# x transposed through DRAM and VectorE, attention's transfers in one piece: one change to a fused layer kernel

## The chip, the cores and the metric

The kernel runs on one core of a Trainium2 chip. TensorE (PE) multiplies, VectorE (DVE) and ScalarE (ACT) work on tensors in SBUF and PSUM, GpSimd (POOL) on SBUF alone, and the DMA queues of SyncE (SP) and ScalarE move data between DRAM and SBUF over 16 DMA engines. The metric is the time of one execution on the device, in microseconds; lower is better.

## The reference

S = 2048 rows of D = 512 are normalized, go through a local attention with 32 heads of 16 (each row looks at itself and the rows 2, 4, ... 14 before it) and through a gated feed-forward part with F = 1792:

```python
def _A_ref(x, wqkv, wo):
    H = 32; Dh = D // H; W, dil = 8, 2
    q, k, v = (x @ wqkv) split into (3, H, Dh)
    idx = pos[:, None] - (jnp.arange(W) * dil)[None, :]
    logits = jnp.einsum("bhsd,bhswd->bhsw", q, k[idx]) * Dh ** -0.5
    logits = jnp.where(idx >= 0, logits, -1e9)
    o = jnp.einsum("bhsw,bhswd->bhsd", softmax(logits), v[idx])
    return o.reshape(B, S, D) @ wo

def _B_ref(x, w1, b1, w2, b2):
    r = relu(x @ w1 + b1)
    return (r * r) @ w2 + b2

xn = _layernorm(x)
out = x + _A_ref(xn, wqkv, wo) * silu(_B_ref(xn, w1, b1, w2, b2))
```

(The code is shortened: reshapes, transposes and the batch of 1 are left out.)

## The kernel before

**Precision.** Each float32 product is made of three products of float32r parts: `high` copies a value rounded to float32r on ScalarE, `low` subtracts it from the value on VectorE or Pool, `split` does both (L105 to L113). `PASSES` (L34) lists the pairs high by high, high by low, low by high.

**Tiles.** A tile t is 128 rows (16 tiles), a chunk c is 4 tiles (512 rows), an attention unit u is 2 tiles (256 rows, 8 units).

**Phase 1** (L435 to L541) goes over the tiles. `mean` and `spread` (L342, L347) get a tile's statistics by ScalarE passes whose full-size result goes to a `scratch` tile in SBUF; `norm(t)` (L354) writes the normalized `xn` and calls `load_x(t + 4)`. `trans(t)` (L373) transposes `xn` on TensorE, four 128x128 blocks into PSUM `pxT`, and ScalarE copies the high part to `xt`; `lowx(t)` (L381) subtracts the low part from PSUM on VectorE. `qkv` (L385) then does 12 products for each of q, k and v, copies the result to `stg` on ScalarE and stores it to DRAM (`sq`, `sk`, `sv`). For tiles 4 to 15 both parts of `xt` are spilled to DRAM `sx` (L538); chunk 0's stay in SBUF (`xT`). At step t of the loop (L507) the code calls `norm(t + 3)`, q's products, `trans(t + 2)`, `spread(t + 4)`, k's products, `mean(t + 5)`, `lowx(t + 2)`, v's products and the spill, in this order. The w1 and w2 blocks of the first six f are loaded and split on the way (`load_w`, `split_w`).

**Phase 2** (L544 to L700) goes over the chunks and, in each, over 14 blocks f of F. `up(c, f)` (L407) is 12 products, then ScalarE makes relu and two squares, and `lowh(f)` (L423) makes the low part on VectorE; `down` (L547) multiplies two f later into four accumulators `pb`. `load_xT` (L400) brings the next chunk's `xT` back from `sx` on ScalarE's DMA queue as soon as the last `up` of a chunk is issued; there is one buffer for it. Between the last `up` of a chunk and the first of the next, TensorE does `down` of f = 11 (12 products), two `out_product` (24), and `down` of f = 12. `gate` adds the bias and applies silu; `trans_o`, `out_product` and `finish` make the attention's output product, multiply and store.

**Attention** (L202 to L292) runs on VectorE beside all this. A unit's q, k and v come from DRAM by `load_u` (L191): the heads lie in 4 groups g, and group g has the partitions 32g to 32g + 31, so each transfer is made of four DMAs over 32 partitions; `store` (L255) writes the result to `so` the same way. Per unit there are 4 products with k (`qk`) and 4 with v (`av`), each a 2048-wide multiplication and reduction, and the softmax.

**What sets the order.** All instructions of the engines keep the order in which the code issues them (`Ordered`, L62); DMAs from SP are not bound to it and are placed by the framework's planner. The code keeps two clocks, one for TensorE and one for VectorE (L49), and adds a price for every instruction: 227 ns a product, 150 a transpose, VectorE's elements at 0.96 per ns and 170. `pump(margin)` (L297) issues the next pieces of attention while VectorE's clock is at most `margin` after TensorE's: LATE = 3000 ns in phase 1, ROOM = 1000 ahead of each `lowh`, -SLACK = -500 elsewhere. `not_before` moves VectorE's clock up to a time at which an operand can be there.

Of the kernel before, what the change touches and what calls it, by code (L numbers as in the profile page):

```python
# [44 lines left out]
def body(ctx: ExitStack, tc: tile.TileContext, x, wqkv, wo, w1, b1, w2, b2, out):  # L45
# [117 lines left out]
    zero = px.tile([HALO, 4, P], F32, name="zero")  # L163

    def constants():
        G.memset(zero, 0.0)
        for t in (sk, sv):
            dma(t[:, :HALO, :].rearrange("g h c -> h g c"), zero)
        G.memset(mask, 0.0)
        for g in range(4):  # L170
            for blk in (1, 0):
                for w in range(W):
                    n = max(0, min(BI, (W - 1 - w) * DIL - blk * BI))
                    if n:
                        G.memset(mask[32 * g:32 * g + blk + 1, :n, w], -1e9)
# [8 lines left out]
    sx = {c: dram.tile([P, TPC, 2, KT, P], F32, name=f"sx{c}") for c in range(1, NCH)}  # L184
# [6 lines left out]
    def load_u(what, u):  # L191
        n = BI if what == "q" else WIN
        src = dict(q=sq, k=sk, v=sv)[what]

        t = att.tile([P, n, P], F32, name=f"{what}{u}", tag="k" if (what, u) == ("v", NU - 1) else what)
        for g in range(4):
            row = src[g, u * UP:u * UP + 1, :]
            ap = bass.AP(tensor=row.tensor, offset=row.offset, ap=[[BI * P, NB], [1, n * P]])
            dma(t[32 * g:32 * g + 32].rearrange("p i c -> p (i c)"), ap)
        return t  # L200

    def attention():  # L202
# [52 lines left out]
        def store(u):  # L255
            v = tiles.pop(("v", u))
            for g in range(4):
                dst = so[g, u * UP:(u + 1) * UP, :].rearrange("(n i) c -> n i c", i=BI)
                dma(dst, v[32 * g:32 * g + 32, :BI, :])
            done_units[0] = u + 1  # L260
# [66 lines left out]
    mv, means, rs, shifts, xn, pTs, xt, xT, seen = {}, {}, {}, {}, {}, {}, {}, {}, {}  # L327
# [11 lines left out]
    def scratch(t):  # L339
        return px.tile([P, D], F32, name=f"scratch{t}", tag="scratch")  # L340
# [13 lines left out]
    def norm(t):  # L354
        xn[t] = px.tile([P, D], F32, name=f"xn{t}", tag="xn", bufs=2)
        if t < 2:
# [10 lines left out]
    def place(t):  # L367
        if t < TPC:
            xt[t] = xT[0][:, t]
        else:  # L370
            xt[t] = pxT.tile([P, 2, KT, P], FR, name=f"xt{t}", tag="xt", bufs=4)

    def trans(t):  # L373
        place(t)
# [63 lines left out]
    high(*wq_parts(0, 0))  # L438
    V.bn_stats(sts[1], xins[1])
    norm(0)  # L440
    moments(1, sts[1])
    low(*wq_parts(0, 0), V)
    high(*wq_parts(0, 1))
    low(*wq_parts(0, 1), G)
    xT[0] = xTa.tile([P, TPC, 2, KT, P], FR, name="xT0", tag="xT")
    place(0)
# [5 lines left out]
    for kt in (0, 2):  # L452
# [3 lines left out]
        V.tensor_sub(lo, src, hi.bitcast(F32))  # L456
    norm(1)
    for kt in (2, 3):
        split(*wq_parts(0, kt), V)
# [10 lines left out]
    def first():  # L470
        trans(1)
        highs(1, 0)

# [5 lines left out]
    mean(2)  # L479
# [27 lines left out]
    for t in range(2, NT):  # L507
# [14 lines left out]
        if t + 5 < NT:  # L522
            mean(t + 5)
# [6 lines left out]
        if t + 2 < NT:  # L530
            lowx(t + 2)
# [5 lines left out]
        if t >= TPC:  # L537
            dma(sx[t // TPC][:, t % TPC], xt.pop(t).bitcast(F32))  # L538
# [70 lines left out]
    for c in range(NCH):  # L609
# [3 lines left out]
        for f in range(2, NF):  # L613
# [51 lines left out]
            pump(ROOM)  # L665
# [4 lines left out]
        if not last:  # L670
            for i in range(2):
# [50 lines left out]
```

## Time and profile before

| | us |
|---|---|
| time, median of 3 runs | 509.35 |
| lowest and highest of them | 506.99, 510.22 |
| the profiled execution's own time | 508.16 |
| its span in the profile | 506.0 |
| granted TensorE clock | 0.999 |

Of the span 2.2 us lie outside it in the profiled execution's own time. Phase 1 runs to about 156 us, then come the chunks. "Busy" is the time in which an engine had an instruction in work; VectorE's and ScalarE's instructions don't overlap much, TensorE's overlap (a product that starts every 227 ns is shown with 389), so its gaps are read from the starts. DMA landings go from the issue to the last byte.

The page's slices of the span, 40 of 12.65 us each, show the three stages: tenths of busy time of the engines, and the DMA engines' share:

```profile
DVE  5309999999999999999699999879998878942235
ACT  3946375663233556431722432182224226223421
POOL 2542256473000369600203000020100002020000
PEclk9999999999999999999999999999999999999999
DMA  8989999899969994937270834644476514021022
```

VectorE is full from the fourth slice on and empties in the last fifth; the DMA engines are full in phase 1 (the first 12 slices) and half used later.

### The profile page before, as it was taken

Reading aid. Unit: us, or ns where it says so; the run is one execution under the profiler, and the core shown is the slowest. Engines: PE = TensorE matmul, PEld = TensorE weight load, DVE = VectorE, ACT = ScalarE, POOL = GpSimd, SP = SyncE. Lnnn points to the kernel's source line nnn. Section 1 sums busy time; section 2 is a strip of 40 time slices with the busy share of each in tenths; the row PEclk is TensorE's granted clock in tenths of the full one; section 3 lists DMA queues with packets and bytes.
Section 4 is the critical chain, followed back from the end, with each engine's and each line's share of the span. In section 5 each row is a group of like instructions: output and inputs, shape, how many; then the busy total and the mean of one; then the engine's idle time right before and its main releaser. Section 6 shows DMA issues by size and latency. Waiting matters only on the chain.

```text
span 506.0 us, 6148 instructions
## 1 busy us (share of the span) xinstructions
PE 496.5 (98%) x2209; PEld 409.2 (81%) x2209; DVE 416.8 (82%) x328; ACT 215.3 (43%) x393; POOL 110.4 (22%) x156
## 2 busy tenths in 40 slices
PE   7999999999999999899999999999999999999997
PEld 6788888888888787688888888888888888888886
DVE  5309999999999999999699999879998878942235
ACT  3946375663233556431722432182224226223421
POOL 2542256473000369600203000020100002020000
PEclk9999999999999999999999999999999999999999
DMA  8989999899969994937270834644476514021022
GB/s 289 284 207 239 263 303 264 216 305 303 267 193 275 268 235 128 218 126 196 85 176 21 200 82 176 147 140 100 123 161 138 182 42 126 0 84 32 10 84 83
DMA packets 63626, 85.67 MB, mean 169 GB/s; under 512 B 6908, under 2 KB 47212, under 8 KB 60780
## 3 DMA queue, kind: packets, MB, share of 16 engines
q1 hardware_dynamic: 62732, 78.99, 58.9%
q10 hardware_dynamic: 864, 6.29, 3.3%
q8 instruction: 17, 0.28, 0.2%
q14 instruction: 13, 0.11, 0.1%
HBM read 57.94 MB, written 27.32 MB: 168 GB/s over the span
## 4 chain that ended last, share of the span: by engine, by line
PE 86%; DMA 7%; DVE 3%; issue 2%; SPq 1%; POOL 1%; ACT 0%; DVEq 0%; POOLq 0%; ACTq 0%
PE pq L74 26%; PE ph L74 25%; PE pb L74 25%; PE pw L74 9%; DMA w2r<-in_B_w 2%; DMA sx<-xt 2%; PE pxT L74 2%; DMA rwo<-in_A_wo 1%; DMA x<-in_A_x 1%; DVE L L74 1%; DMA q<-sq 1%; DVE pr L74 1%; DMA w1r<-in_B_w 1%; POOL w L74 1%; DVE h L74 0%
## 5 line engine op out<-in xcount | busy, mean ns | idle before, releaser
L74 PE MATMUL pb<-w,h 128*128 128x512 f32 x672 | 161.1, 389 | 0.0
L74 PEld LDWEIGHTS pb<-w,h 128*128 128x128 f32 x672 | 126.1, 188 | 26.2
L74 PE MATMUL ph<-xU,w 128*128 128x512 f32 x504 | 120.6, 389 | 0.0
L74 ACT ACTIVATE ph<-ph,b1t 128x512 f32<-128x512 f32 x56 | 37.0, 660 | 192.9 <-PE ph L74 183.4
L74 PEld LDWEIGHTS ph<-xU,w 128*128 128x128 f32 x504 | 94.6, 188 | 19.6
L74 PE MATMUL pq<-wq,xt 128*128 128x512 f32 x432 | 101.3, 392 | 0.0
L74 PEld LDWEIGHTS pq<-wq,xt 128*128 128x128 f32 x432 | 80.3, 188 | 16.4
L74 DVE TENSOR_TENSOR pr<-k,q 128x2048 f32<-128x2048 f32 x32 | 76.9, 2403 | 12.9 <-DMA k<-sk 12.4
L74 DVE TENSOR_TENSOR h<-ph,h 128x512 fp32r<-128x512 f32 x56 | 38.3, 684 | 44.3 <-ACT ph L74 44.3
L74 DVE TENSOR_TENSOR pv<-v,L 128x2048 f32<-128x2048 f32 x32 | 74.0, 2311 | 0.5
L74 DVE TENSOR_REDUCE v<-pv 128x256 f32<-128x2048 f32 x32 | 73.0, 2282 | 0.8
L74 DVE TENSOR_REDUCE L<-pr 128x128 f32<-128x2048 f32 x32 | 73.0, 2281 | 0.7
L74 POOL TENSOR_TENSOR z<-z,xr 128x512 f32<-128x512 f32 x12 | 19.2, 1615 | 218.8 <-DVE z L74 179.2
L74 PE MATMUL pw<-wot,oT 128*128 128x512 f32 (+1 forms) x204 | 45.5, 376 | 0.0
L74 ACT ACTIVATE stg<-pq 128x512 f32<-128x512 f32 x48 | 28.3, 597 | 35.9 <-PE pq L74 20.7
L74 PE MATMUL ph<-xT,w 128*128 128x512 f32 x168 | 41.2, 394 | 2.0 <-DVE h L74 1.9
L74 PEld LDWEIGHTS pw<-wot,oT 128*128 128x128 f32 x204 | 36.8, 188 | 7.1
L74 PEld LDWEIGHTS ph<-xT,w 128*128 128x128 f32 x168 | 31.1, 188 | 10.5 <-DVE h L74 4.0
L74 PE MATMUL pq<-wq,xT 128*128 128x512 f32 x144 | 36.9, 414 | 0.0
L74 POOL TENSOR_TENSOR w<-w1r,w 128x512 fp32r<-128x512 f32 x14 | 22.6, 1616 | 59.0 <-DMA w2r<-in_B_w 47.8
L74 ACT ACTIVATE h<-ph 128x512 fp32r<-128x512 f32 x56 | 33.7, 602 | 1.7
L74 ACT ACTIVATE ph<-ph 128x512 f32<-128x512 f32 x56 | 33.3, 595 | 0.0
(54 smaller groups left out, 323.8 us busy)
## 6 DMA issues: line engine op xcount, KB each, us to landing
k<-sk SPq DMA_DIRECT2D x32, 352.0 KB, 6.5
v<-sv SPq DMA_DIRECT2D x32, 352.0 KB, 5.6
sx<-xt SPq DMA_DIRECT2D x12, 512.0 KB, 6.7
xU<-sx ACTq DMA_DIRECT2D x6, 1024.0 KB, 7.1
x<-in_A_x SPq DMA_DIRECT2D x16, 256.0 KB, 5.5
sq<-stg SPq DMA_DIRECT2D x16, 256.0 KB, 6.0
q<-sq SPq DMA_DIRECT2D x32, 128.0 KB, 3.4
sk<-stg SPq DMA_DIRECT2D x16, 256.0 KB, 5.6
```

Of the source, the lines that this page charges most:

```text
L74: return tc.keep_in_program_order(f(*a, **k))
```

## The change

For the tiles 4 to 15 TensorE's transposes go. `norm(t)` writes `xn` with its columns permuted (the four 32-wide pieces of each 128 columns are sorted by piece), SP stores it to a DRAM tile `sn`, and four DMAs of 32 partitions each bring it back as `xb`, so that each 32x32 block lies in the partitions where its transpose belongs. `turn(t)` transposes all 32x32 blocks in one VectorE instruction into `xf`, and `parts(t)` splits `xf`, the high part on ScalarE, the low part on Pool, and spills `xf` itself as float32 to `sx`, half the bytes of before. `load_xT` then loads float32 into the place of the low parts, and `split_xT` splits it in place, the low parts on VectorE and Pool in turn. At step t the loop now calls `norm(t + 4)` ahead of q's products, `parts(t + 1)` behind them, and `turn(t + 2)` behind k's products.

```diff
-    sx = {c: dram.tile([P, TPC, 2, KT, P], F32, name=f"sx{c}") for c in range(1, NCH)}
+    sx = {c: dram.tile([P, TPC, KT, P], F32, name=f"sx{c}") for c in range(1, NCH)}
+    sn = {t: dram.tile([P, 4, P], F32, name=f"sn{t}") for t in range(TPC, S // P)}
...
         else:
-            A.activation(xn[t], xins.pop(t), AF.Identity, bias=shifts.pop(t), scale=rs[t])
+            A.activation(xn[t].rearrange("p (a k c) -> p k a c", a=4, k=KT),
+                         xins.pop(t).rearrange("p (k a c) -> p k a c", a=4, k=KT),
+                         AF.Identity, bias=shifts.pop(t), scale=rs[t])
+            dma(sn[t].rearrange("p a c -> p (a c)"), xn.pop(t))
+            xb[t] = px.tile([P, 4, P], F32, name=f"xb{t}", tag="xb", bufs=3)
+            for a in range(4):
+                dma(xb[t][32 * a:32 * a + 32], sn[t][:, a].rearrange("(b p) c -> p b c", p=32))
...
+    def turn(t):
+        xf[t] = px.tile([P, KT, P], F32, name=f"xf{t}", tag="xf", bufs=2)
+        V.transpose(out=xf[t].rearrange("p k (b n) -> p b k n", n=32),
+                    in_=xb.pop(t).rearrange("p b (k c) -> p b k c", k=KT))
+
+    def parts(t):
+        f = xf.pop(t)
+        xt[t] = pxT.tile([P, 2, KT, P], FR, name=f"xt{t}", tag="xt", bufs=3)
+        split(xt[t][:, 0], xt[t][:, 1], f, G)
+        dma(sx[t // TPC][:, t % TPC], f)
...
-            A.dma_start(xT[c][:, j:j + 2].bitcast(F32), sx[c][:, j:j + 2])
+            A.dma_start(xT[c][:, j:j + 2, 1].bitcast(F32), sx[c][:, j:j + 2])
+
+    def split_xT(c):
+        for j in range(TPC):
+            hi, lo = (xT[c][:, j, i] for i in range(2))
+            split(hi, lo, lo.bitcast(F32), V if j % 2 == 0 else G)
...
-        if t + 3 < NT:
-            norm(t + 3)
+        if t == 2:
+            norm(5)
+        elif t + 4 < NT:
+            norm(t + 4)
         qkv_tile(t, 0)
-        if t + 2 < NT:
-            trans(t + 2)
-        if t + 4 < NT:
-            spread(t + 4)
+        if t == 2:
+            spread(6)
+            norm(6)
+        if TPC <= t + 1 < NT:
+            parts(t + 1)
+        if t > 2 and t + 5 < NT:
+            spread(t + 5)
         pump(LATE)
...
-        if t + 2 < NT:
-            lowx(t + 2)
+        if TPC <= t + 2 < NT:
+            turn(t + 2)
         pump(LATE)
         qkv_tile(t, 2)
-        if t >= TPC:
-            dma(sx[t // TPC][:, t % TPC], xt.pop(t).bitcast(F32))
```

Attention's transfers become one DMA each over all 128 partitions: the partition of a row block n and a head group g is now 4n + g instead of 32g + n, and the mask follows that order, with a quarter of the memsets.

```diff
-        for g in range(4):
-            row = src[g, u * UP:u * UP + 1, :]
-            ap = bass.AP(tensor=row.tensor, offset=row.offset, ap=[[BI * P, NB], [1, n * P]])
-            dma(t[32 * g:32 * g + 32].rearrange("p i c -> p (i c)"), ap)
+        row = src[0, u * UP:u * UP + 1, :]
+        ap = bass.AP(tensor=row.tensor, offset=row.offset, ap=[[BI * P, NB], [src.shape[1] * P, 4], [1, n * P]])
+        dma(t.rearrange("p i c -> p (i c)"), ap)
```

In phase 2 chunk 0's margin ahead of `lowh` changes, and at the end of a chunk `split_xT` and both last `down` come ahead of the next chunk's two `up`, and `lowh(0)` behind the gates:

```diff
-            pump(ROOM)
+            pump(ROOM if c else -SLACK)
             lowh(f)
...
                 for j in range(TPC):
                     down(pb, NF - 2 + i, j)
                 pump()
-                if i:
-                    lowh(0)
+                if i == 0:
+                    split_xT(c + 1)
+            for i in range(2):
                 up(c + 1, i)
             for j in range(TPC):
                 gate(c, j, pb)
+            lowh(0)
             lowh(1)
             pump()
```

In the start, which the diff above leaves out, `norm(0)` comes ahead of tile 1's `bn_stats`, the low part of the first weight block goes from VectorE to Pool and that of the second from Pool to VectorE, the third block's goes to Pool, and `mean(2)` moves from ahead of the first products to behind tile 1's transposes and two weight copies on ScalarE. `scratch`, the full-size result of `mean` and `spread` that nothing reads, moves from SBUF to the two PSUM buffers of `pxT`; `zero` shares the buffers of `xf`; `xt` has three buffers instead of four.

More of the change, by code (lines that the diff above doesn't have):

```diff
@@ L162, in body @@
     mask = const.tile([P, BI, W], F32, name="mask")
-    zero = px.tile([HALO, 4, P], F32, name="zero")
+    zero = px.tile([HALO, 4, P], F32, name="zero", tag="xf", bufs=2)
     def constants():
@@ L169, in constants @@
         G.memset(mask, 0.0)
-        for g in range(4):
[L171 to L175, printed above, removed]
+        for blk in (1, 0):
+            for w in range(W):
+                n = max(0, min(BI, (W - 1 - w) * DIL - blk * BI))
+                if n:
+                    G.memset(mask[:4 * blk + 4, :n, w], -1e9)
     b1t = const.tile([P, NF], F32, name="b1t")
@@ L326, in body @@
     NT = S // P
-    mv, means, rs, shifts, xn, pTs, xt, xT, seen = {}, {}, {}, {}, {}, {}, {}, {}, {}
+    mv, means, rs, shifts, xn, xb, xf, pTs, xt, xT, seen = ({} for _ in range(11))
     def moments(t, st):
@@ L339, in scratch @@
     def scratch(t):
-        return px.tile([P, D], F32, name=f"scratch{t}", tag="scratch")
+        return psT(f"scratch{t}")
     def mean(t):
@@ L456, in body @@
         V.tensor_sub(lo, src, hi.bitcast(F32))
+        if kt == 0:
+            high(*wq_parts(0, 1))
+    low(*wq_parts(0, 1), V)
     norm(1)
-    for kt in (2, 3):
-        split(*wq_parts(0, kt), V)
+    split(*wq_parts(0, 2), G)
+    split(*wq_parts(0, 3), V)
     clock.update(PE=8000.0, V=10000.0)
@@ L472, in first @@
         highs(1, 0)
+        mean(2)
     def second():
@@ L477, in second @@
         norm(3)
-    mean(2)
     qkv_tile(0, 0, first)
@@ L521, in body @@
         qkv_tile(t, 1)
-        if t + 5 < NT:
-            mean(t + 5)
+        if t == 2:
+            mean(7)
+            spread(7)
+        if t + 6 < NT:
+            mean(t + 6)
         if t == NT - 1:
```

24 lines of the change are left out of this document (9 added, 15 removed).

## The prediction

> **What bounds the kernel now.** I read the page first, its busy times and the chain of waits.
>
> ```profile
> PE 496.5 (98%) x2209; PEld 409.2 (81%) x2209; DVE 416.8 (82%) x328; ACT 215.3 (43%) x393; POOL 110.4 (22%) x156
> ...
> PE 86%; DMA 7%; DVE 3%; issue 2%; SPq 1%; POOL 1%; ACT 0%; DVEq 0%; POOLq 0%; ACTq 0%
> PE pq L74 26%; PE ph L74 25%; PE pb L74 25%; PE pw L74 9%; DMA w2r<-in_B_w 2%; DMA sx<-xt 2%; PE pxT L74 2%; DMA rwo<-in_A_wo 1%; DMA x<-in_A_x 1%; DVE L L74 1%; DMA q<-sq 1%; DVE pr L74 1%; DMA w1r<-in_B_w 1%; POOL w L74 1%; DVE h L74 0%
> ```
>
> TensorE is the bound: it sets 86% of the chain, so what is taken out of its queue comes off the time, unless another engine falls in behind it. The same chain in order of time (start, length, what) shows the piece that the change takes out:
>
> ```profile
> 33.04 0.44 PE pxT L74 x4
> ...
> 120.16 8.19 PE pq L74 x36
> 128.34 0.44 PE pxT L74 x4
> ```
>
> These are the four transposes of a tile, between 36 products that follow each other without a gap. The first row belongs to tile 4, the last to tile 15; there are 12 such entries. Then I looked for TensorE's gaps, in its timeline from 156 us on (start, length with the modelled end, operation, idle before):
>
> ```profile
> 158.82 2.88 PE L74 MATMUL pb<-w,h 128*128 128x512 f32 x12
> 161.54 2.88 PE L74 MATMUL ph<-xT,w 128*128 128x512 f32 x12
> ...
> 213.77 3.02 PE L74 MATMUL ph<-xT,w 128*128 128x512 f32 x12 [1.31 <-DVE h L74]
> ```
>
> A group of 12 products starts every 2.72 us (161.54 less 158.82) when nothing stalls. From 158.82 to 213.77 stand 19 groups, which would take 51.7 us; they took 54.95. So 3.3 us are lost in chunk 0, and the last row names VectorE's `lowh` as the one waited for. The busy times by stretch (us; PE, PEld, DVE, ACT, POOL; clock; DMA share, GB/s) say why VectorE comes late there:
>
> ```profile
> 41.00:145.00 104.00, 104.00 (x481) 85.98 (x480) 102.10 (x64) 54.73 (x113) 40.49 (x51) 1.00 0.98 272
> 145.00:217.00 72.00, 69.98 (x303) 56.22 (x302) 71.41 (x47) 35.57 (x63) 34.59 (x20) 1.00 0.83 206
> ```
>
> VectorE is busy 98% and 99%, so a delay it takes in the first stretch is carried into the second. The DMA engines are full in the first stretch too (0.98), and the clock is 1.00: no gain or loss can come from it.
>
> **Part by part.** *TensorE's transposes.* 12 tiles by 0.44 us: **-5.3 us**, all on the path.
>
> *VectorE's work for the same tiles* is exchanged one for one; the groups by form, with the mean in ns last before the idle time:
>
> ```profile
> L74 DVE STREAM_TRANSPOSE pT<-oq 128x512 f32<-128x512 f32 x16 | 10.5, 699 | 0.0
> ...
> L74 DVE TENSOR_TENSOR xt<-pxT,xt 128x512 fp32r<-128x512 f32 x12 | 8.2, 682 | 0.0
> ```
>
> `turn` is a block transpose of the size in the first row, `lowx` the second: 12 x 0.02 = +0.2 us of VectorE. Its row transposes into PSUM and the new one into SBUF; between equal and the 2.29 us of a 2048-wide pass lies everything I can exclude, and I take equal.
>
> *VectorE's lateness in chunk 0.* The plan prices a transpose at 150 ns, 0.60 us a tile, where the row has 0.44; over 12 tiles it gives VectorE 1.9 us of attention more than TensorE's time has room for. Without transposes that goes. `pump(ROOM)` with 1000 ns becomes -500 in chunk 0: 1.5 us more. And attention starts late; the waits name the cause (total, times, longest):
>
> ```profile
> DVE pr L74 <- DMA k<-sk: 12.4, 1, 12.4
> ```
>
> That is the first k, in four pieces. What one piece over all partitions is worth, two stretches show: one just after the four pieces of a later k were issued, one with the load of `xlast` over 128 partitions (columns as before, DMA share and GB/s last):
>
> ```profile
> 232.50:238.50 6.00, 6.00 (x28) 4.99 (x27) 5.93 (x4) 1.75 (x3) 0.00 (x0) 1.00 1.05 227
> ...
> 484.00:488.00 4.00, 4.00 (x20) 3.30 (x19) 2.61 (x4) 1.73 (x4) 0.00 (x0) 1.00 0.80 258
> ```
>
> At a full share that is 216 against 322 GB/s, so a unit's k (4 x 352 KB, 1.44 MB) takes 4.5 us of the engines instead of 6.7. Up to 2.2 us of the 12.4 go. Together 3.4 to 5.6 us less lateness against 3.3 us of stalls; against it stand up to 4 us that `turn(4)` may wait (below). I take **-2.3 us**, bounds -3.3 and 0.
>
> *Pool's 12 new subtractions in phase 1.* What Pool costs VectorE, the groups from 145 to 217 us and the instructions that read k (min/median/max) show:
>
> ```profile
> L74 DVE TENSOR_TENSOR pr<-k,q 128x2048 f32<-128x2048 f32 x7 | 18.5, 2646 | 0.1
> ...
> L74 POOL TENSOR_TENSOR w<-w2r,w 128x512 fp32r<-128x512 f32 x8 | 14.9, 1862 | 0.0
> ```
>
> ```profile
> L74 DVE TENSOR_TENSOR pr<-k,q x32: 2275/2291/3376, 39.1 to 383.6; 128x2048 f32<-128x2048 f32 x32
> ```
>
> With Pool busy 34.6 of 72 us, seven `pr` lost 0.36 us each over the median, 2.5 us. Twelve subtractions at 1.86 us add 22 us of Pool in 104 us; in proportion 2.5 x 22/34.6 = 1.6 us of VectorE, covered by the lateness removed above, nothing on TensorE's path. [...]
>
> *The way through DRAM.* The sizes and landings:
>
> ```profile
> k<-sk SPq DMA_DIRECT2D x32, 352.0 KB, 6.5
> v<-sv SPq DMA_DIRECT2D x32, 352.0 KB, 5.6
> sx<-xt SPq DMA_DIRECT2D x12, 512.0 KB, 6.7
> xU<-sx ACTq DMA_DIRECT2D x6, 1024.0 KB, 7.1
> x<-in_A_x SPq DMA_DIRECT2D x16, 256.0 KB, 5.5
> sq<-stg SPq DMA_DIRECT2D x16, 256.0 KB, 6.0
> q<-sq SPq DMA_DIRECT2D x32, 128.0 KB, 3.4
> ```
>
> A tile adds `sn` out and `xb` in, 256 KB each, and halves `sx`: +256 KB, 0.9 us at the stretch's 278 GB/s (272/0.98). A unit of attention saves 2 x 2.2 = 4.4 us for about five tiles, 4.7 us added: the queue stays as full as it is. ScalarE's pass of `norm` (min/median/max):
>
> ```profile
> L74 ACT ACTIVATE xn<-x,shift,rs x14: 800/806/829, 18.4 to 121.3; 128x512 f32<-128x512 f32 x14
> ```
>
> The round trip: two such passes, 1.6 us, until `norm(t+4)` is done; 6.0 for `sn` (the `sq` row); four issues at 0.4 (SP's rows below); `xb` 3.4 to 6.0, from the `q` row's 32-partition pieces to the `sq` row: 13 to 15 us. `turn(t+4)` stands two steps and two thirds later, 2.67 x 8.19 = 22 us. Hidden, with some 7 us to spare, for all but tile 4, which is normalized while the first q and k load; there I allow VectorE 0 to 4 us, counted above.
>
> *The split after each reload.* The issues of `xU` and the first product that reads it (ScalarE's timeline, then TensorE's):
>
> ```profile
> 222.26 1.02 ACTq L74 DMA_DIRECT2D xU<-sx  x2
> ```
>
> ```profile
> 232.94 2.88 PE L74 MATMUL ph<-xU,w 128*128 128x512 f32 x12
> ```
>
> The cover is 10.7 us; `down` of the last f moves ahead of `up(c+1, 0)` and makes it 13.4. Needed: at most 7.1 for half the bytes, four ScalarE passes of at most 0.81, one Pool subtraction of 1.86: 12.2. Hidden by 1.2; with an attention load (4.5) ahead of it 3.3 would show. Then `lowh(0)` sits behind four gate additions, and `up` twice in a row leaves one group instead of two to hide it. Bounds 0 to 3.3 for each of three; I take **+0.3 each, +0.9**, near the lower end, because a load of half the bytes should not need the 7.1 of the whole.
>
> *The start.* Pool and VectorE change places on the first weights, `norm(0)` no longer waits behind `bn_stats(1)`, `mean(2)` comes later on ScalarE. The product there already waits for ScalarE:
>
> ```profile
> 19.29 0.66 PE L74 MATMUL pxT<-ident,xn 128*128 128x128 f32 x4 [0.60 <-ACT xn L74]
> ```
>
> That chain (x2, mean, spread, norm) decides, not the earlier steps. From -1.0 (the gap of 0.60 gone, and some of the wait before the first product) to +1.6 (two ScalarE passes ahead of it); I take **-0.4**.
>
> **Sum**: -5.3 - 2.3 + 0.9 - 0.4 = -7.1 on the profiled execution's 508.16: 501.1. The median of the three runs, 509.35, is 1.2 higher: **502** to the nearest. Mask, `zero` and statistics into PSUM cost nothing that TensorE waits for.
>
> **Rivals.** *Slower: SP becomes the bound.* If SP keeps the order of the calls, `xb` stands behind the landing of `sn`, and everything behind that. SP's timeline (start, length):
>
> ```profile
> 11.09 0.39 SPq L317 DMA_DIRECT2D w1r<-in_B_w  x1
> ...
> 78.05 0.38 SPq L127 DMA_DIRECT2D x<-in_A_x  x1
> 78.52 0.40 SPq L397 DMA_DIRECT2D sq<-stg  x1
> ```
>
> A step then has ten issues at 0.4 and 6.0 of waiting: 10.0 us against TensorE's 8.19, and 10.8 in the six steps with weight loads. Ten steps: 4 x 1.8 + 6 x 2.6 = 23 us late, 7 of them spare: +16 - 5.3 on 509.35 gives **520**. It decides from a wait of 4.2 us (8.19 less 4.0) on. For it: the landings of 5.5 to 6.7. Against: SP does not keep that order (the first row is a weight load called at tile 5, issued at 11 us), so x and `sq` can go ahead of `xb`, and a wait lets the full queue drain. 0.19.
>
> *No change: VectorE is the bound of the front half.* At 98 and 99% busy it may simply hand TensorE's gain back as a longer wait in chunk 0: lost are 1.6 us to Pool, 4 at `turn(4)`, and xT's splits; a sum of 6 takes the 5.3 back: **509 to 510**. For it: the stretches. Against: the plan emits attention by TensorE's clock, so a shorter phase 1 carries less of it, and VectorE is free later. 0.13. [...]
>
> That the freed 5.3 us don't show at all I exclude: the transposes stand gapless in the chain.
>
> **How the numbers follow.** Forecast 0.68; its own range is -5.3 - 3.3 - 1.0 + 0 = -9.6, 499.7, to -5.3 + 0 + 0.9 + 1.6 = -2.8, 506.6; three boundaries at their upper bound would add 9 to the forecast, 511. One per cent (5.1 us, about what this kernel's runs can tell) puts the borders at 504.3 and 514.4: of the 0.68 some 0.56 lie under the first. Faster 0.56, same 0.12 + 0.13 = 0.25, slower 0.19. The range from 499 to 511 holds the forecast and the VectorE case and leaves out the SP case.
>
> **What would show it.** Right: `pxT` x16 instead of x64; no `lowh` wait over 0.5 us in chunk 0; k landing in some 5 us; TensorE starting a new chunk without idle time. Wrong: `turn` waiting for `xb` on more than tile 4, `stg` waits on ScalarE longer than a step, or idle time of TensorE on `xt` in phase 1 (the SP case); `lowh` waits of several us up to 217 us (the VectorE case).

## The result, and the profile after

The changed kernel takes 516.82 us (median of four runs, 516.22 to 517.81) beside 509.79 for the kernel before (four runs, 506.99 to 510.34): ratio 1.0162, 95% interval 1.0134 to 1.019. It is slower, and lies above the whole range forecast. The profiled execution took 516.83 with a span of 515.0, 9.0 us longer than before, and a mean granted TensorE clock of 0.987 (1 is full speed).

From the page of the changed kernel, the shares of the chain of waits by engine and by line:

```profile
PE 81%; DMA 5%; issue 4%; POOL 3%; ACT 3%; DVE 2%; SPq 1%; ACTq 0%; POOLq 0%; DVEq 0%
PE ph L74 30%; PE pb L74 30%; PE pq L74 13%; PE pw L74 8%; DMA sv<-stg 1%; DMA sx<-xf 1%; DMA w2r<-in_B_w 1%; POOL xt L74 1%; ACT stg L74 1%; ACT scratch L74 1%; DVE L L74 1%; POOL rs L74 1%; DMA x<-in_A_x 1%; DMA sn<-xn 1%; DVE pr L74 1%
```

TensorE has 48 instructions fewer, the 12 x 4 transposes, and yet its share of the chain fell from 86 to 81%: ScalarE and Pool, 0 and 1% before, now hold 3% each. Phase 1's products (`pq`) fell from 26 to 13% of the chain, because the chain now goes through what they wait for.

**Phase 2 gained more than was forecast.** The first `ph` starts at 156.62 in the changed kernel (in the timeline below); before, by TensorE's timeline:

```profile
144.97 2.94 PE L74 MATMUL ph<-xT,w 128*128 128x512 f32 x12
```

From there to the end of the span it took 361.0 us before and 358.4 after, 2.6 less, where the forecast had -2.3 + 0.9 = -1.4. In chunk 0 no group waits for `lowh` any more, and the first three groups of a new chunk cost 0.17 over 8.16, as the changed kernel's chain shows:

```profile
244.07 8.33 PE ph L74 x36
```

**Phase 1 lost 11.65 us although 5.3 us of work were gone.** TensorE's timeline of the changed kernel (start, length, operation, idle before and what ended it) has its stalls in three places, the first products of the tiles 4, 10 and 13:

```profile
40.79 6.29 PE L74 MATMUL pq<-wq,xT 128*128 128x512 f32 x24 [0.24 <-ACT stg L74]
50.18 0.87 PE L74 MATMUL pq<-wq,xt 128*128 128x512 f32 x2 [3.10 <-ACT xt L74]
51.54 49.96 PE L74 MATMUL pq<-wq,xt 128*128 128x512 f32 x214 [0.48 <-POOL xt L74]
103.16 0.73 PE L74 MATMUL pq<-wq,xt 128*128 128x512 f32 x2 [1.66 <-ACT xt L74]
104.52 25.94 PE L74 MATMUL pq<-wq,xt 128*128 128x512 f32 x106 [0.63 <-POOL xt L74]
135.23 21.56 PE L74 MATMUL pq<-wq,xt 128*128 128x512 f32 x84 [4.76 <-ACT xt L74]
156.62 2.94 PE L74 MATMUL ph<-xT,w 128*128 128x512 f32 x12
```

Each time TensorE waits for ScalarE's high part of `xt`, and twice, two products later, for Pool's low part. From 40.79 to 156.62 stand 432 products, which at 8.19/36 = 0.2275 us would take 98.3; they took 115.8. So 17.6 us are lost; less the 5.3 of the transposes and the 0.9 by which this execution's start was shorter that is 11.4 of the 11.65. The idle times in the brackets on `xt` sum to 10.6. The windows around the stalls show where most of the rest is (columns as before: the stretch, PE, PEld, DVE, ACT, POOL, granted clock, DMA share, GB/s):

```profile
50.00:52.00 2.00, 1.33 (x3) 0.76 (x4) 2.00 (x2) 2.00 (x7) 1.70 (x2) 0.66 1.00 271
52.00:54.00 2.00, 2.00 (x6) 1.54 (x6) 1.97 (x2) 0.42 (x1) 1.92 (x2) 0.50 0.66 217
...
105.00:107.00 2.00, 2.00 (x7) 1.56 (x6) 1.97 (x2) 2.00 (x4) 1.92 (x4) 0.56 1.08 443
107.00:109.00 2.00, 2.00 (x7) 1.54 (x6) 1.97 (x2) 0.48 (x2) 2.00 (x1) 0.59 1.07 372
...
135.00:137.00 2.00, 1.64 (x3) 0.92 (x4) 1.14 (x2) 1.15 (x3) 1.28 (x1) 0.50 0.67 162
137.00:139.00 2.00, 2.00 (x6) 1.54 (x6) 1.97 (x2) 0.00 (x0) 0.00 (x0) 0.50 0.83 243
139.00:141.00 2.00, 2.00 (x10) 1.60 (x9) 2.00 (x1) 0.48 (x1) 0.00 (x0) 0.91 1.01 315
```

Around each stall the granted clock is 0.50 for a while, by windows of 0.1 us from 50.6 to 54.0, from 105.2 to 108.7, and from 132.5, 2.7 us ahead of the first product after the stall, to 139.4. TensorE is shown busy all the same (2.00 of 2.00 us from 52 to 54, 105 to 109 and 137 to 139). Each window's length times what its clock lacks to 1 gives 1.7 us lost after the first stall, 1.7 after the second and 2.2 after the third, 5.6 in all. (The pace of the products agrees: the 84 after the third took 156.62 - 135.23 = 21.4 us instead of 19.1.) Idle and slow clock make 16.2 of the 17.6; a stall is also a little longer than its bracket, since a bracket counts from the modelled end of the product before (0.389 us after its start by the page's mean, where products that nothing stalls start every 0.2275).

**Why ScalarE came late.** Its timeline shows three long waits ahead of the three late copies of `xt`:

```profile
40.14 0.60 ACT L74 ACTIVATE stg<-pq 128x512 f32<-128x512 f32 x1 [8.41 <-DMA sv<-stg]
...
49.51 0.62 ACT L74 ACTIVATE xt<-xf 128x512 fp32r<-128x512 f32 x1
...
100.77 0.63 ACT L74 ACTIVATE L<-L 128x512 f32<-128x512 f32 x1 [6.79 <-DVE L L74]
...
102.49 0.62 ACT L74 ACTIVATE xt<-xf 128x512 fp32r<-128x512 f32 x1
...
114.18 0.60 ACT L74 ACTIVATE stg<-pq 128x512 f32<-128x512 f32 x1 [1.08 <-PE pq L74]
...
134.06 0.60 ACT L74 ACTIVATE stg<-pq 128x512 f32<-128x512 f32 x1 [11.12 <-DMA sv<-stg]
134.55 0.62 ACT L74 ACTIVATE xt<-xf 128x512 fp32r<-128x512 f32 x1
```

`stg` has two buffers, one per tile, so ScalarE's first copy of a tile waits until `sv` of the tile two before has landed. The other wait is attention's Exp (`L`), which waits for VectorE. Everything behind either stands still, the copy of `xt` included; after the first, at 40.14, ScalarE needs another nine us for the normalization passes of the next tiles, with waits of 1.23 and 1.70 for Pool, before that copy's turn comes. The first long wait is not new. ScalarE's timeline before has it too, and the copy of tile 4's `xt` stands right behind it, at 40.48:

```profile
39.99 0.60 ACT L74 ACTIVATE stg<-pq 128x512 f32<-128x512 f32 x1 [7.31 <-DMA sv<-stg]
```

Why `sv` lands so late ahead of the third stall, SP's timeline says (issues, with their lengths):

```profile
114.67 0.43 SPq L411 DMA_DIRECT2D sv<-stg  x1
...
116.36 0.42 SPq L369 DMA_DIRECT2D sn<-xn  x1
116.88 0.38 SPq L411 DMA_DIRECT2D sq<-stg  x1
...
121.05 2.73 SPq L372 DMA_DIRECT2D xb<-sn  x4
124.57 0.54 SPq L198 DMA_DIRECT2D v<-sv  x1
125.21 0.54 SPq L411 DMA_DIRECT2D sk<-stg  x1
125.85 0.45 SPq L411 DMA_DIRECT2D sv<-stg  x1
```

The `sv` issued at 125.85 stores what ScalarE had copied at 114.18. It stood behind four `xb` loads, which had themselves waited for `sn`, issued at 116.36, to land, and behind a 1408 KB load of v. ScalarE's wait of 11.12 ends 8.2 us after that issue, at 134.06. Over the whole run SP's waits (total, times, longest) show how long it stood still at `xb` for `sn`:

```profile
SPq L372 <- DMA sn<-xn: 25.6, 11, 6.1
```

The waits of `turn`, at which the prediction had looked for trouble, are small. The view of the waits (total, times, longest) has for `xb`, and for the first k:

```profile
DVE pr L74 <- DMA k<-sk: 12.3, 1, 12.3
...
DVE xf L74 <- DMA xb<-sn: 1.1, 1, 1.1
```

With the waits that the view puts down to other DMAs, `turn` waited five times, 10.2 us in all, and none of them ends a stall of TensorE. (The largest, 4.08 us, is put down to `sx`: `xf` has two buffers, and one is free only when its spill has landed.)

### The profile page after: what moved, and what is told of

Read it like the earlier page. It is cut to its first block, busy times and chain, and to the rows that moved or that the text cites. A ratio compares the mean times of both kernels' runs of the same rounds, so it can differ in the third digit from the quotient of the medians.

```text
span 515.0 us, 6030 instructions
## 1 busy us (share of the span) xinstructions
PE 495.9 (96%) x2161; PEld 406.0 (79%) x2161; DVE 428.0 (83%) x333; ACT 224.5 (44%) x407; POOL 139.4 (27%) x145
## 3 DMA queue, kind: packets, MB, share of 16 engines
q1 hardware_dynamic: 69836, 82.13, 50.6%
## 4 chain that ended last, share of the span: by engine, by line
PE 81%; DMA 5%; issue 4%; POOL 3%; ACT 3%; DVE 2%; SPq 1%; ACTq 0%; POOLq 0%; DVEq 0%
PE ph L74 30%; PE pb L74 30%; PE pq L74 13%; PE pw L74 8%; DMA sv<-stg 1%; DMA sx<-xf 1%; DMA w2r<-in_B_w 1%; POOL xt L74 1%; ACT stg L74 1%; ACT scratch L74 1%; DVE L L74 1%; POOL rs L74 1%; DMA x<-in_A_x 1%; DMA sn<-xn 1%; DVE pr L74 1%
## 5 line engine op out<-in xcount | busy, mean ns | idle before, releaser
L74 PE MATMUL pq<-wq,xt 128*128 128x512 f32 x432 | 104.8, 404 | 10.8 <-ACT xt L74 9.5
L74 PEld LDWEIGHTS pq<-wq,xt 128*128 128x128 f32 x432 | 83.9, 195 | 31.4 <-ACT xt L74 10.8
L74 DVE TENSOR_TENSOR pr<-k,q 128x2048 f32<-128x2048 f32 x32 | 77.8, 2430 | 12.9 <-DMA k<-sk 12.3
L74 DVE TENSOR_TENSOR pv<-v,L 128x2048 f32<-128x2048 f32 x32 | 76.5, 2390 | 0.4
L74 DVE TENSOR_TENSOR h<-ph,h 128x512 fp32r<-128x512 f32 x56 | 38.4, 686 | 32.4 <-ACT ph L74 32.3
L74 POOL TENSOR_TENSOR z<-z,xr 128x512 f32<-128x512 f32 x12 | 17.3, 1456 | 120.3 <-DVE z L74 79.2
L74 POOL TENSOR_TENSOR xU<-xU 128x512 fp32r<-128x512 f32 x6 | 11.6, 1948 | 92.3 <-ACT xU L74 92.2
```

The lines of the kernel that those rows point to most:

```text
L74: return tc.keep_in_program_order(f(*a, **k))
```

## The experiments

The theory after this reading: the stall is ScalarE's copy of `xt`, which `parts(t + 1)` makes two thirds of a step before TensorE needs it (1.67 steps before the change), and it comes late because stores wait on SP behind `xb`'s wait for `sn`. Rivals: the short lead alone, whatever SP does; the Exp; the new traffic on full DMA engines; Pool's subtractions, by their time or by what they take from VectorE. Ratios are to the kernel before on the same chip.

| run | what differs | us | ratio, 95% interval |
|---|---|---|---|
| `one_piece` | before, attention's transfers in one piece | 506.03 | 0.9946 (0.992 to 0.9971) |
| `four_piece` | after, those transfers in four pieces | 531.13 | 1.0426 (1.0385 to 1.0466) |
| `lead` | after, `turn` and `parts` two thirds of a step earlier | 513.61 | 1.0093 (1.0062 to 1.0124) |
| `xb_late` | after, `xb` issued behind the step's stores | 511.70 | 1.0060 (1.0036 to 1.0085) |
| `lead_xb_late` | both | 510.50 | 1.0033 (1.0014 to 1.0051) |
| `exp_late` | after, Exp three products later | 515.82 | 1.0148 (1.0124 to 1.0171) |
| `lead_xb_exp` | all three | 513.76 | 1.0114 (1.0089 to 1.0139) |
| `short_lead` | before, with the short lead | 508.83 | 1.0025 (1.0006 to 1.0045) |
| `xb_p4` | `xb` late from tile 6, `parts(4)` earlier | 509.36 | 1.0020 (0.9996 to 1.0045) |
| `xb_exp_p4` | the same and Exp later | 507.40 | 0.9989 (0.9969 to 1.0009) |
| `xb_p4_lead9` | `xb_p4`, longer lead from tile 9 | 509.50 | 1.0033 (1.0013 to 1.0053) |
| `one_margin` | `one_piece`, `pump(-SLACK)` in chunk 0 | 506.39 | 0.9975 (0.9955 to 0.9996) |
| `no_wait` | after, `xb` from `x`, no wait for `sn` | 506.59 | 0.9966 (0.9942 to 0.9990) |
| `pool_free` | after, no low parts on Pool | 517.40 | 1.0170 (1.0144 to 1.0196) |
| `no_wait_pool_exp` | `no_wait`, `pool_free` and Exp later | 504.28 | 0.9923 (0.9907 to 0.9940) |

`no_wait`, `pool_free` and `no_wait_pool_exp` don't compute the reference's output; what they leave out is said there. Of the ranges that the theory gave ahead of the runs only those of `one_piece` and `no_wait` held. `short_lead` lost less than expected, and every other kernel was slower than its range: by 0.5% or less in eight, by 0.7 to 1.9% in `lead_xb_late`, `xb_p4_lead9`, `lead` and `lead_xb_exp`. The theory has the places right and the price of mending them wrong, because a mended wait uncovers another.

### The two halves of the change

`one_piece` puts the second diff of the change into the kernel before; `four_piece` takes it out of the changed kernel.

```diff
-        for g in range(4):
-            row = src[g, u * UP:u * UP + 1, :]
...
+        row = src[0, u * UP:u * UP + 1, :]
...
+        dma(t.rearrange("p i c -> p (i c)"), ap)
```

> The kernel before with nothing but attention's transfers in one piece each (and the mask in that order of partitions). Theory A: this half of the change is harmless; TensorE's work is the same, its stalls of 3.3 us in chunk 0 shrink by at most that, ratio to before 0.993 to 1.000. Rival: 1.4 MB in one issue blocks the queue for the stores behind it, and this half alone costs 2 us or more, ratio above 1.004.

> The changed kernel with attention's transfers in four pieces again (and the old mask): x through DRAM alone. Theory A: the three stalls stay, and with a DMA queue fuller by some 4 us of engine time a unit the waits for sv's store get longer; ratio to before 1.015 to 1.04. Rival (the single pieces cause the stalls): the stalls go, ratio 0.985 to 0.995.

`one_piece` is 0.5% faster than before, the fastest version here that computes everything. Its windows show the relief in the DMA engines, 0.87 of the first stretch against 0.98, with TensorE as full as before:

```profile
41.00:145.00 104.00, 104.00 (x480) 86.05 (x479) 102.10 (x62) 51.65 (x106) 40.61 (x47) 1.00 0.87 286
```

Where its 0.5% comes from is not shown. Of the 2.0 us between the two profiled spans 1.2 lie in the start (third transpose at 18.12 instead of 19.29), and `short_lead`, with the start and the transfers of the kernel before, has that too (18.10).

The other half alone costs 4.3%. The two don't add: 1.0426 times 0.9946 would be 1.037, not 1.016. One piece saves three issues per transfer on SP, and engine time, and is worth far more beside the first half (2.6% between 1.0426 and 1.0162) than alone (0.5%). That fits a queue which the first half has made critical: in `four_piece` ScalarE's waits for `sv` sum to 38.4 us, in the changed kernel to 19.5.

### Which wait makes the copy late

`lead` moves both new steps two thirds of a step ahead; `xb_late` leaves the lead and lets the stores of a step go first:

```diff
+        if TPC <= t + 2 < NT:
+            turn(t + 2)
         qkv_tile(t, 0)
...
-        if TPC <= t + 1 < NT:
-            parts(t + 1)
...
         if TPC <= t + 2 < NT:
-            turn(t + 2)
+            parts(t + 2)
```

```diff
             dma(sn[t].rearrange("p a c -> p (a c)"), xn.pop(t))
-            xb[t] = px.tile([P, 4, P], F32, name=f"xb{t}", tag="xb", bufs=3)
-            for a in range(4):
-                dma(xb[t][32 * a:32 * a + 32], sn[t][:, a].rearrange("(b p) c -> p b c", p=32))
...
         qkv_tile(t, 2)
+        if t == 2:
+            fetch(5)
+            fetch(6)
+        elif t + 4 < NT:
+            fetch(t + 4)
```

(`fetch(t)` holds the lines taken out.)

> The changed kernel with turn(t + 2) called at the start of step t and parts(t + 2) behind k's products, so ScalarE's copy of a tile stands 1.33 steps ahead of its first product instead of 0.67. Theory A (the lost lead: ScalarE stands still 7 to 11 us at a time for stg's buffers and for the Exp behind VectorE, and a lead of 5.5 us no longer covers that while 11 us would): TensorE's three stalls of phase 1 go nearly, some 17 us of idle time and lowered clock, time 500 to 504 us. Theory B (SP's queue behind the landing of sn is too slow whatever the lead): the stalls come later but stay, 510 us or more. Theory C (VectorE late through Pool's subtractions): turn stands earlier in its queue but attention is pushed back as much, 512 to 517 us.

> The changed kernel with the four xb loads of a tile called at the end of the step whose start stores sn, behind the stores of q, k and v, so that SP no longer waits for sn's landing ahead of them. Theory A: ScalarE's wait for sv's store before tile 13's copy (11.1 us) shrinks below the lead and that stall of some 5 us with its slow clock goes; the first one stays in part, because sv's store also stands behind the first k, and the one behind the Exp stays; time 505 to 511 us. Theory B: all three go, 499 to 503 us. Theory C: no change, 515 to 518 us.

`lead` takes back 0.7 of the 1.6%. TensorE's timeline of this kernel shows why not more: ScalarE's copy of `xt` is no longer late, but its long waits for `sv` are still there, and now stop TensorE through the copy that empties PSUM (`stg`), 8.5 us in four stalls.

```profile
50.38 0.72 PE L74 MATMUL pq<-wq,xt 128*128 128x512 f32 x2 [1.81 <-ACT stg L74]
...
134.03 18.93 PE L74 MATMUL pq<-wq,xt 128*128 128x512 f32 x72 [4.37 <-ACT stg L74]
```

`xb_late` takes back 1.0%. SP waits far less for `sn` (its waits first), and the stall near 134 is gone; those of tile 4 and of the Exp stay, as its TensorE timeline says:

```profile
SPq L376 <- DMA sn<-xn: 6.7, 6, 2.5
...
50.16 0.73 PE L74 MATMUL pq<-wq,xt 128*128 128x512 f32 x2 [3.75 <-ACT xt L74]
...
105.49 0.99 PE L74 MATMUL pq<-wq,xt 128*128 128x512 f32 x2 [2.79 <-ACT xt L74]
```

`exp_late` lets three products of attention go ahead of the Exp, and two kernels combine the edits; `short_lead` gives the kernel before the lead of the changed one, with its transposes still on TensorE:

```diff
             V.tensor_sub(L, L, mx[:, :, None].to_broadcast([P, BI * 8, W]))
-            A.activation(L, L, AF.Exp)
+
+        def exp(u):
+            A.activation(Ls[u], Ls[u], AF.Exp)
...
                     yield from av(max(u - 1, 0), s)
+                    if 0 < u < NU and s == 2:
+                        exp(u)
```

```diff
         qkv_tile(t, 0)
-        if t + 2 < NT:
-            trans(t + 2)
+        if TPC <= t + 1 < NT:
+            trans(t + 1)
+            lowx(t + 1)
...
-        if t + 2 < NT:
-            lowx(t + 2)
```

> Both edits on the changed kernel: xb loaded behind the stores, and turn and parts two thirds of a step earlier. Each left the other's stall alone (with the lead alone ScalarE still stood 10.7 us for sv's store; with the late loads alone its copy still came late behind the Exp, 7.9 us). Theory A: they add up, the stall behind the Exp and the one near 130 us both go, the first one at 40 to 50 us stays in part; 503 to 507 us. Rival (with xb later and turn earlier the round trip itself is too long): VectorE waits for xb at turn, 5 us or more in sum at several tiles, and the time stays at 509 or more.

> The changed kernel with softmax's Exp issued on ScalarE some three attention products later (behind the third product with v instead of straight behind VectorE's subtraction; unit 0 as before). Theory A: ScalarE no longer stands 6.8 us for VectorE ahead of a tile's copy, the stall at 102 us of some 2.5 us and the slow clock behind it go, 3 to 5 us less than the changed kernel, 512 to 514 us. If that wait were not what delays the copy: 516 to 518 us.

> All three edits on the changed kernel. Theory A: nothing is left in phase 1 but the first stall, at 40 to 50 us (sv's store behind the first k), worth 3 to 6 us; 499 to 504 us, under the kernel before. If Pool or VectorE is the cause instead, no better than either edit alone, 509 us or more.

> The kernel before, its transposes on TensorE, with nothing but the lead of the changed kernel: trans(t + 1) and lowx(t + 1) behind q's products of step t instead of trans(t + 2) there and lowx(t + 2) a third of a step later. No tile goes through DRAM to be transposed. Theory A: ScalarE's waits that before shows too (7.3 us for sv's store, 6.1 us behind the Exp) now stop TensorE, ratio to before 1.01 to 1.04. If the way through DRAM is what costs the time: 0.995 to 1.005.

`exp_late` removes the stall at 103 and gains no more than its interval is wide, because a new stall comes at 118 and the last one grows from 4.76 to 5.77:

```profile
118.18 0.73 PE L74 MATMUL pq<-wq,xt 128*128 128x512 f32 x2 [0.34 <-ACT xt L74]
120.13 8.00 PE L74 MATMUL pq<-wq,xt 128*128 128x512 f32 x34 [1.22 <-POOL xt L74]
133.90 22.16 PE L74 MATMUL pq<-wq,xt 128*128 128x512 f32 x84 [5.77 <-ACT xt L74]
```

`lead_xb_late` is better than `lead`, hardly more than its interval better than `xb_late`, and still 0.3% slower than before; VectorE now waits 15.4 us for the `xb` of the earlier `turn(4)`. `lead_xb_exp`, which adds the later Exp, is worse than without it (513.76 against 510.50); a wait of 3.95 us for `lowh` at 162.51 appears in chunk 0. Why that `lowh` comes so late was not followed further.

`short_lead` rejects the short lead as a cause by itself: with it the kernel before loses 0.25%, and TensorE has no stall in phase 1 although ScalarE waits 7.75 us for `sv` and 4.78 and 2.94 for the Exp. So something has to come on top of the short lead. At the tiles 10 and 13 it is a longer wait, 6.79 us for the Exp and 11.12 for `sv`. At tile 4 it is not the wait (8.41 us against the 7.75 here, and the 6.94 of `no_wait` below also ends in a stall) but what ScalarE does after it: the changed kernel's `norm` runs a tile further ahead, and the copy comes 9.4 us after the end of the wait (40.14 to 49.51), in `short_lead` 4.0 (39.64 to 43.59).

Three more kernels look for what placement alone can give. `xb_p4` issues `xb` late only from tile 6 on, so that tile 4 is not held up, and calls `parts(4)` right behind `turn(4)`:

```diff
+            if t < 6:
+                fetch(t)
...
-        if TPC <= t + 1 < NT:
+        if TPC < t + 1 < NT:
             parts(t + 1)
...
+        if t == 2:
+            parts(4)
         pump(LATE)
         qkv_tile(t, 2)
+        if t + 4 < NT:
+            fetch(t + 4)
```

(In `fetch(t + 4)` t is 2 or more.) `xb_exp_p4` adds the later Exp, `xb_p4_lead9` the longer lead for the tiles from 9 on.

> The late xb loads from tile 6 on (tiles 4 and 5 at once, as in the changed kernel), and tile 4's parts moved from step 3 to straight behind its turn in step 2, ahead of a step's worth of ScalarE's statistics. Theory D (three queues in order now carry x: SP with the landing of sn ahead of the stores, ScalarE with its waits and statistics ahead of the copy, VectorE with attention ahead of turn; each stall has its own place): the first stall, 3.8 + 0.6 us and the slow clock behind it in the run with late loads alone, goes; 506 to 508 us. Rival (the first stall is sv's store behind the first k, whatever ScalarE does next): 511 to 513 us.

> As xb_p4, with the Exp issued three attention products later. Theory D: the second stall (2.8 + 0.4 us behind the Exp) goes too; 502 to 505 us. Rival (the Exp only moves the stall: softmax's second half on VectorE then waits, and lowh in chunk 0 stops TensorE as it did with all three edits): no better than xb_p4.

> As xb_p4, with turn and parts two thirds of a step earlier from tile 9 on, where the queues have settled, and the Exp in its old place. Theory D: the copy stands ahead of the Exp's wait; no xb wait at turn over 1 us; 502 to 506 us. Rival (turn earlier makes VectorE wait for xb, as it did 15.4 and 4.7 us at tiles 4 and 5 with the lead everywhere): 509 us or more.

With `parts(4)` ahead, tile 4's stall shrinks from 3.75 and 0.63 us in `xb_late` to 1.70 and 0.27 in `xb_p4`, and the 1.70 is now a wait for `stg`; the Exp's stall stays, 3.13. In `xb_p4_lead9` that one is gone, and new gaps of 2.00 us for Pool's `xt` and 1.85 for `stg` take its place. `xb_exp_p4` is the best of the three, 1.7% under the changed kernel and level with the kernel before. Its granted clock from 41 to 145 us is 1.00, so no slow clock is left there. But TensorE's small gaps in its phase 1 (1.64 on `stg`, 0.98 on ScalarE's `xt`, 2.67 on Pool's) sum to 5.3 us, the very amount that the transposes had taken. That the two amounts are equal is chance, but with the placement mended as far as these runs go, x's way through DRAM buys nothing, and `one_piece` without it has the lower ratio, 0.9946.

### The causes one by one

`no_wait` loads `xb` from the input, so that no issue waits for `sn`, while every byte still moves; its tiles 4 to 15 are not normalized. `pool_free` takes Pool's subtraction away and multiplies the high part in place of the low one.

```diff
-                dma(xb[t][32 * a:32 * a + 32], sn[t][:, a].rearrange("(b p) c -> p b c", p=32))
+                dma(xb[t][32 * a:32 * a + 32],
+                    x[t * P:(t + 1) * P, a * P:(a + 1) * P].rearrange("(b p) c -> p b c", p=32))
```

```diff
-        split(xt[t][:, 0], xt[t][:, 1], f, G)
+        high(xt[t][:, 0], None, f)
...
-                PE.matmul(ps, xt[t][:, a, kt], wq[s][:, b, kt, :], start=n == 0, stop=n == 11)
+                PE.matmul(ps, xt[t][:, a if t < TPC else 0, kt], wq[s][:, b, kt, :], start=n == 0, stop=n == 11)
```

> The changed kernel with xb loaded from the input x, in packets of the same size, instead of from sn; sn is still stored, and nothing waits for it. The output is not the reference's: tiles 4 to 15 multiply columns of x that are neither normalized nor in place. Theory D: SP's wait is the largest of the three causes; the stall near 130 us goes and the first one in part, 506 to 512 us, near the late xb loads. Rival (the traffic of 0.5 MB a tile, not the wait, fills the queues): 514 us or more.

> The changed kernel without Pool's subtraction for tiles 4 to 15; their product with the low part takes the high part in its place, so TensorE's work is the same and the output less exact. Theory D: Pool is the smallest cause, 0.3 to 0.6 us of TensorE at each stall and some 2 us of VectorE; 513 to 516 us. Theory C (Pool makes VectorE late and so ScalarE and x): 510 us or less.

> Both of these and the Exp three attention products later, on the changed kernel; the output is not the reference's for the same reasons. If the three account for the stalls: 498 to 503 us, the removed transposes and chunk 0's stalls then show as forecast. If something else of x's way stops TensorE: 506 us or more.

`no_wait` is 2.0% faster than the changed kernel (0.9966 against 1.0162), some 10 us and more than the whole loss, with the same traffic. So SP's wait for `sn`, with what stands behind it, is the cause of most of it, and the traffic is not. (`no_wait` takes the round trip's own time away as well; in the changed kernel VectorE waited 1.1 us for it.) The first `ph` starts at 147.35 instead of 156.62. What is left of SP's waits for `sn`, and its TensorE timeline:

```profile
SPq L412 <- DMA sn<-xn: 0.7, 2, 0.6
...
49.22 1.22 PE L74 MATMUL pq<-wq,xt 128*128 128x512 f32 x2 [3.17 <-ACT xt L74]
51.49 50.37 PE L74 MATMUL pq<-wq,xt 128*128 128x512 f32 x214 [1.05 <-POOL xt L74]
102.78 0.74 PE L74 MATMUL pq<-wq,xt 128*128 128x512 f32 x2 [0.92 <-ACT xt L74]
104.14 43.37 PE L74 MATMUL pq<-wq,xt 128*128 128x512 f32 x190 [0.62 <-POOL xt L74]
```

The stall of tile 13 is gone, that of tile 10 shrinks to 0.92 and 0.62, and that of tile 4 stays: there ScalarE waits 6.94 us for an `sv` that SP had not held back for `sn`. (The kernel before has that wait too, 7.31 us, with tile 4's copy right behind it and not behind the passes of further tiles.) No run moves `xb` to another engine's queue, with the stores left on SP's.

`pool_free` is no faster than the changed kernel (1.0170 against 1.0162). The stalls are where they were, only now on ScalarE's copy alone:

```profile
50.34 16.61 PE L74 MATMUL pq<-wq,xt 128*128 128x512 f32 x72 [2.99 <-ACT xt L74]
...
102.62 26.62 PE L74 MATMUL pq<-wq,xt 128*128 128x512 f32 x108 [2.51 <-ACT xt L74]
135.62 21.86 PE L74 MATMUL pq<-wq,xt 128*128 128x512 f32 x84 [6.37 <-ACT xt L74]
```

In the changed kernel Pool's part comes 1.3 us behind ScalarE's, and TensorE's third product waited 0.48 and 0.63 us for it. Those waits are gone here, but the last stall grew from 4.76 to 6.37 us, so that a gain below the width of the intervals can't be excluded. Nor is Pool's part free: in `xb_exp_p4`, where the rest is mended, Pool's `xt` ends half of the gaps (2.67 of 5.3 us).

`no_wait_pool_exp` is 0.6 to 0.9% under the kernel before, 3 to 5 us. Left there are 2.19 us on tile 4, 1.65 on `lowh` at 155.65 and a clock of 0.98 in the first stretch. So even with all three causes away x's way gives back part of the 5.3 + 2.6 us taken out of TensorE's time.

### The margin in chunk 0

```diff
-            pump(ROOM)
+            pump(ROOM if c else -SLACK)
             lowh(f)
```

> The kernel before with attention's single pieces and chunk 0's margin of -500 ns ahead of lowh, nothing of x's way through DRAM. With single pieces alone TensorE lost 1.9 us in chunk 0; if VectorE's lateness there is what the margin covers, most of that goes: 0.5 to 2 us under the single pieces alone, ratio to before 0.990 to 0.994. If not, 0.994 to 0.996.

The kernel with one-piece transfers loses no group in chunk 0 with this margin, but the gain is lost again at the next chunk: in TensorE's timeline the wait for `xU`, 0.34 us in `one_piece`, is now 2.00 (at 230.22).

## Why the prediction was wrong

**TensorE's transposes, -5.3: right.** 48 instructions are gone, and nothing else in phase 1's products changed.

**VectorE's lateness in chunk 0, -2.3: right in size, half wrong in its reasons.** The 3.3 us of `lowh` stalls are gone. One of the three reasons fell: the first k lands no earlier, VectorE's wait for it is 12.3 after 12.4. The load itself is 1.9 us shorter, near the 2.2 of the forecast (issued at 30.77 and used at 38.75, before at 29.18 and 39.10), but it is issued 1.6 us later. A k in one piece takes 7.5 us (median) from issue to landing, not some 5. The margin was a real reason: in `one_margin` it alone removes what `one_piece` had left in chunk 0. In the changed kernel VectorE may also have gained time while TensorE stood still; how much of the 3.3 that alone would have removed, no run separates.

**The split after each reload, +0.9: too high.** A boundary costs 0.17 us, some 0.5 for three. **The start, -0.4: not shown.** The third transpose comes at 18.35 instead of 19.29, but `short_lead`, whose start is that of the kernel before, has it at 18.10. So the 0.9 is a difference between executions and not the edit's.

**Pool, nothing on the path: right within the intervals,** by `pool_free`. VectorE's loss is near the forecast: the 32 `pr` take 77.8 us with the subtractions and 75.5 in `pool_free`, 2.3 us where 1.6 were forecast. The subtractions themselves take 1270 to 3003 ns each.

**The way through DRAM: this step failed.** It put the cost in phase 1 at nothing, and 17.6 us were lost there. "Hidden, with some 7 us to spare, for all but tile 4" compared the round trip with the time of `turn`, and that was nearly right: `turn` waited for `xb` once, 1.1 us, at tile 5. But the round trip's waiting time is spent on SP, 25.6 us in 11 waits, ahead of `sk` and `sv`, and those stores free the buffers that ScalarE needs before it reaches `xt`. Without that wait the kernel is 2.0% faster (`no_wait`), more than the whole loss. The working asked when the data would be back and not what stands in line while SP waits for it. The step also left out what the new order does on ScalarE: `parts` stands one step nearer to TensorE's use than the old `trans`, and for tile 4 behind the passes of further tiles, so that a delay which was hidden before (7.31 us at 39.99) became a stall. With the short lead alone it did not (`short_lead`).

**The rival "SP becomes the bound", at 0.19, had the mechanism,** stores behind `xb`'s wait for `sn`, but not the size of it. Its price for phase 1, 16 us lost, is close to the 17.6 measured by luck: it took a wait of 6.0 us in every step and said that it decides from 4.2 on, and the 25.6 us measured are 2.3 a wait. SP did not fall behind step by step; single stores were held back long enough (that of 125.85 by 11 us) to stop ScalarE. And it had neither the 5.6 us of slow clock nor the gain of phase 2. Two arguments had put it down. "SP does not keep that order" is true and didn't help: `sq` goes ahead of `xb` at 116.88, but `sk` and `sv` don't. "A wait lets the full queue drain" looks at the engines, not at the line. The DMA share of the first stretch did fall, from 0.98 to 0.90, as the changed kernel's row for it shows (the clock is the third number from the end, the share the second), and landings grew shorter, `sq`'s from 6.0 to 4.1 us in the median, and still the stores stood behind the wait:

```profile
41.00:145.00 104.00, 93.08 (x381) 74.09 (x381) 91.94 (x58) 52.55 (x108) 58.34 (x62) 0.93 0.90 276
```

**"No gain or loss can come from" the clock: wrong.** It held for the kernel before, whose clock is 1.00 from 41 to 217 us and where TensorE never waits longer than 1.31 us there. In the changed kernel a clock of 0.50 stands around each of the three stalls, and the 5.6 us that it costs come on top of the 10.6 of idle time.

**VectorE as the bound** did not happen: 41 to 145 us show it 91.9 us busy instead of 102.1, and 10.2 of the 12.1 us without work are the waits of `turn`.

## What to carry to other kernels

When an edit sends data out and back through DRAM, as this one does, the load back can hold up what stands behind it on its queue (here SP stood 25.6 us in 11 waits for `sn`, and an `sv` went out 11 us after ScalarE had its data): list what is issued behind it in that time, which buffers those DMAs free, and which engine stands still for them, before asking whether the data itself is in time. A step that moves from one engine to another is priced with its new lead as well, the distance to its first use against the longest wait that the new engine shows anywhere in that stage. And two edits that load the same queue are to be measured apart: here one alone is 0.5% faster, and together with the other it hid three fifths of that one's cost.

## What the runs showed of the hardware

Around each of the changed kernel's three stalls in phase 1 TensorE's granted clock was 0.50 for a while: 3.4 us (50.6 to 54.0), 3.5 (105.2 to 108.7) and 6.9 (132.5 to 139.4). The idle time ahead of it does not tell alone when this happens. At 103 it was 1.66 us, two products and 0.63 us, while 0.92 and 0.62 in `no_wait` at the same place left the clock at 1.00 (its window from 100 to 120 us). In `pool_free` 2.99 us ahead of 50.34 left the pace of the products at full (72 in 16.61 us; at 0.2275 from start to start, and 0.39 for the last, 16.5), and 2.51 ahead of 102.62 in the same execution did not (108 in 26.62, where that pace gives 24.7). What decides was not shown.

Of attention's loads in the changed kernel, by the page's DMA issues, a k takes 7.5 us and a v 6.8 from issue to landing (medians of eight, 1408 KB each). One piece lands later than each of the four of 352 KB did from its own issue (6.5 and 5.6), and not much sooner than the last of the four, which is issued some 1.4 us after the first (the first k's four issues take 1.81 us in the kernel before, 0.45 each). What one piece changes clearly is the engines' time, 0.87 against 0.98 of the first stretch in `one_piece`, and the number of SP's issues.
